# One fp32 product per batch, written straight into its layout, in place of a product per head pair that transfers rearrange: attention and two MLPs on one core

## The chip, the cores and the metric

One Trainium2 chip, one core. The metric is the device time in microseconds (us) of one launch. Three runs of the kernel before give the median that later times are compared with; the profile is one further execution. A measurement of this kernel tells differences of about 0.2% (1.4 us) from no change.

## The reference, cut to what matters

```python
B, H, S, Ns, D = 4, 8, 512, 32, 64
scores = x @ state.T / sqrt(D);  a = softmax(scores)        # 512 x 32 for each batch and head
xread = a @ state                                           # 512 x 64
scores2 = state @ x.T / sqrt(D); a2 = softmax(scores2)
sread = a2 @ x                                              # 32 x 64
x = concat([xread, sread]) -> (B * 544, 512)                # 2176 rows, all heads side by side
h = x @ w_in;  x = softplus(h) @ w_out                      # 512 -> 2048 -> 512
h = x @ w_in2; y = (max(h, 0) + alpha * min(h, 0)) @ w_out2 # 512 -> 2048 -> 512
```

## The kernel before, in words

The kernel never forms `xread`. Since xread @ w_in = a @ (state @ w_in), it makes for each batch b (4) and each quarter g of the first MLP's 2048 columns (512 columns, 4 quarters) a matrix M(b, g) = state @ w_in: 256 rows (8 heads of 32 states) by 512 columns. A tile `step1(g, b, fc)` (token `ugbf` of the program) then multiplies 128 columns of M by the attention `at` of the batch (6 matmuls of 128x128x512 into a PSUM bank `ph`), and after softplus (line 582) and a split (253, 254) the result goes through the second weights `wo` in 12 more matmuls of the same size into the four banks `pa`. There are 64 such tiles; the 128 rows of `sread` take a path of their own (`S`), and a second MLP follows (`second_mlp`), with 7 products instead of 8 by a Strassen-like scheme.

All large matmuls are in fp32r, in three passes: each operand is kept as a rounded high half and the low rest. `split` makes the two: ScalarE (ACT) copies to fp32r (line 253), VectorE (DVE) subtracts (line 254). Weights arrive as 64-bit words and are decoded by two ACT and two DVE passes per chunk (`decode`, lines 322 to 328).

How M is made before: for each quarter g and each pair of heads c, `heads_of_m` (token `hgc`) multiplies the split states of all four batches (`stm`) by the split weights `wi`: six matmuls 64x128x512 (line 546) into the two banks `px`; ACT copies both to `tf` (line 551). `make_m` (token `mbg`) then moves the rows of one batch with four transfers from `tf` to `mt` or `mu`, so that a batch's heads come to lie below each other, and splits the result into one of three slots `m` (`NM = 3`). Only M(0, 0) is made otherwise, by `make_first_m` (token `F`): eight fp32 matmuls of 64x32x512, one for each head, each with its own 64 rows and 32 columns of TensorE's array, straight into the layout of M, from weights that are decoded but not split (`wf`):

```python
for c in range(KC):
    for e in range(2):
        T.matmul(PH[ps[e]][32 * c:32 * c + 32, :], state_of(0, c, e), wf(c)[64 * e:64 * e + 64], start=True, stop=True)
```

The scores of a batch (token `s`, line 432) are made in the same form. Line 451 turns them, the softmax runs on DVE and ACT (454 to 461 and 482 to 486), lines 470 and 503 turn them again, and line 517 reads `sread`.

What sets the order: a string `PROGRAM` lists the steps. Each step adds its instructions to a graph with an estimated cost, and `Graph.order` emits them engine by engine, by due times that are worked out backward from TensorE's (PE's) list. Where that plan has PE idle at the start, it puts in filler matmuls with the identity (line 1048). On the chip every engine then runs its own list strictly in order. All transfers are issued from SyncE's queue (SP).

Of the kernel before, what the change touches and what calls it, by code (L numbers as in the profile page):

```python
# [22 lines left out]
P = 128  # L23
# [3 lines left out]
NG = 4  # L27
# [4 lines left out]
NGS = 3  # L32
NM = 3
NST = 3
# [156 lines left out]
def dve_us(n, fast=False):  # L191
    return n / (1920.0 if fast else 960.0) + 0.069
# [3 lines left out]
def attention_then_mlps_kernel(ctx: ExitStack, tc: tile.TileContext, xT, xn, st, w1i, w1o, w2i, w2o, alpha, out):  # L196
# [23 lines left out]
    AT = [lambda b=b: part(f"at{b}", None, F32R) for b in range(B)]  # L220
    STM = part("stm", None, F32R, 1024)
    SR = part("sr", None, F32R, 1024)
    MB = [lambda i=i: part(f"m{i}", None, F32R) for i in range(NM)]
    TF = part("tf", None, F32, 4096)
    MF = [part(t, None, F32, 1024) for t in ("mt", "mu")]
# [15 lines left out]
    def ring(name, n):  # L241
        count[name] = count.get(name, -1) + 1
        return count[name] % n
# [37 lines left out]
    chunk = [0] * (2 * NG)  # L281
    first_in = []

    def wf(c):
        return WF()[:, c * FW:(c + 1) * FW]

    def weight_chunk(g):
        c = chunk[g]
        chunk[g] += 1
        if c < KC:  # L290
            src, dst, key = w1i[c * P:(c + 1) * P, g * FW:(g + 1) * FW], [lambda j=j, c=c: wi_ap(g, j)[:, c, :] for j in range(2)], ("wi", g % 2, c)
        else:
            c -= KC
            src, dst, key = w1o[(g * FC + c) * P:(g * FC + c + 1) * P, :], [wo_ap(g, j)[:, c, :] for j in range(2)], ("wo", g % 2, c)
        extra = chunk[g] - 1 if g == 0 and chunk[g] > NST and chunk[g] <= KC else None
        whole = g == 0 and key[0] == "wi"
        fk = ("wi", 1, c, "hi")
        floats, fks = decode(src, extra, c if whole else None)[:2]
        if whole:
            first_in.append(lambda: split(dst[0], dst[1], lambda: wf(c), 512, [fk], [key]))  # L300
        else:
            split(dst[0], dst[1], floats, 512, fks, [key],
                  also=[("wi", 1, x, "hi") for x in range(KC)] if key[:2] == ("wi", 1) and g == 1 else [])

# [9 lines left out]
    def decode(src, extra=None, whole=None):  # L314
# [12 lines left out]
              [q(2), q(3)], [q(0), q(1)])  # L327
        G.add(DVE, dve_us(512), lambda: V.scalar_tensor_tensor(out=words()[:, :, 1] if whole is None else wf(whole).bitcast(U32), in0=words()[:, :, 1], scalar=3,
                                                              in1=words()[:, :, 0], op0=ALU.logical_shift_left, op1=ALU.bitwise_or),
              [q(0), q(1), q(2), q(3)], [q(2), q(3)] if whole is None else [("wi", 1, whole, "hi")])  # L330
        return floats, [q(2), q(3)], lambda: t().bitcast(F32).rearrange("p (f t) -> p f t", t=2)[:, :, 0], [q(0), q(1)]
# [42 lines left out]

    stm = STM.rearrange("p (j c f) -> p j c f", j=2, c=KC)
    stf = XF[B].rearrange("p (c f) -> p c f", c=KC)
    srt = SR.rearrange("p (j c f) -> p j c f", j=2, c=KC)
    att = lambda b: AT[b]().rearrange("p (j h s) -> p j h s", j=2, h=2)

    def load_state():  # L380
        load(stf, st, [("xf", B)], nbytes=P * 2048)

    def state_of(b, c, e):
        return stf[64 * e:64 * e + 64, c, 32 * (b ^ c):32 * (b ^ c) + 32]

    def split_state():
        split(stm[:, 0], stm[:, 1], stf, 512, [("xf", B)], [("stm",)])

# [9 lines left out]
    def attention(b):  # L398
# [26 lines left out]
        def scores():  # L425
# [8 lines left out]

            G.add(PE, 1.2, mm, xtk + [("xf", B)], [ps[0][1], ps[1][1]], load=0.7)
            for e in range(2):
# [71 lines left out]
        def read():  # L508
# [10 lines left out]

            G.add(PE, 2.4, mm, xsk + szk[2:], [pk], load=0.24)  # L520
            for e in range(2):
# [16 lines left out]

    def heads_of_m(g, c):
        banks = [ring("px", 2) for _ in range(2)]  # L540

        def mm():
            for k, (x, y) in enumerate(PAIRS):
                for e in range(2):
                    r = slice(64 * e, 64 * e + 64)
                    T.matmul(PX[banks[e]], stm[r, x, c, :], wi_ap(g, y)[r, c, :], start=k == 0, stop=k == 2)  # L546

        G.add(PE, 3 * MM + 0.24, mm, both(("stm",), ("wi", g % 2, c)), [("px", i) for i in banks])
        for e in range(2):
            dst = TF[:, (2 * c + e) * 512:(2 * c + e + 1) * 512]  # L550
            G.add(ACT, act_us(512, True), lambda dst=dst, i=banks[e]: A.activation(dst, PX[i], AF.Copy), [("px", banks[e])], [("tf", c, e)])  # L551

    def make_m(b, g):
        s = mslot[b, g] = ring("m", NM)
        if (b, g) == (2, 0):
            G.add(SP, 0.0, lambda: None, [], both(*[("m", s, x, y) for x in range(2) for y in range(2)]))
        i = ring("mf", 2)
        mf = MF[i].rearrange("p (h f) -> p h f", h=2)
        tf = TF.rearrange("p (c h f) -> p c h f", c=KC, h=2)
# [3 lines left out]
        for hg in range(2):  # L563
            split(lambda hg=hg: m_ap(s)[:, 0, hg, :], lambda hg=hg: m_ap(s)[:, 1, hg, :], mf[:, hg, :], 512, [("mf", i, hg, q) for q in range(4)],
                  [("m", s, hg, 0), ("m", s, hg, 1)])

    def make_first_m():
        s = mslot[0, 0] = ring("m", NM)
        ps = [ring("ph", 2) for _ in range(2)]
# [123 lines left out]
    def claim(name, keys):  # L693
        if name not in claimed:
# [8 lines left out]
    srk = both(*[("sr", b, j) for b in range(B) for j in range(2)])  # L703
    XS = [("wi0_0", wik(0, 0)), ("wi1_0", wik(0, 1)), ("wo0_0", wok(0, 0)), ("wo1_0", wok(0, 1)), ("at0", atk(0)), ("tf", [("tf", c, e) for c in range(KC) for e in range(2)]),
          ("at1", atk(1)), ("xf0", [("xf", 0, c) for c in range(KC)])]
# [5 lines left out]
    TS["u"] = [("st0", [("st", 0, k) for k in range(4)]), ("st1", [("st", 1, k) for k in range(4)])]  # L711
    TT = [("sbb", [("st", NST - 1, k) for k in range(4)]), ("sr", srk), ("mt", [("mf", 0, x, q) for x in range(2) for q in range(4)])]

# [296 lines left out]
    def run(plan):  # L1010
        units = [c for c in plan.split() if c[0] == "u"]
        n = -1
        for c in plan.split():
            if c[0] == "z":
                convert()
            elif c[0] == "w":
                weight_chunk(int(c[1]))
            elif c == "F":
                make_first_m()
            elif c[0] == "v":  # L1020
                first_in.pop(0)()
            elif c[0] == "m":
                make_m(int(c[1]), int(c[2]))
            elif c[0] == "h":
                heads_of_m(int(c[1]), int(c[2]))
            elif c[0] == "t":
                load_state()
            elif c[0] == "p":
                split_state()
            elif c[0] == "X":  # L1030
# [24 lines left out]

PROGRAM = "w0 n w0 w0 t0 w0 F v0 w0 p0 i0 j0 s0 h00 v0 w0 v0 r0 c0 l1 u000 s1 k0 u001 u002 w0 h02 b0 v0 w1 u003 h03 x0 h01 c1 r1 w0 w1 b1 x1 l2 m10 u100 m20 u101 s2 r2 c2 u102 u103 w1 b2 u200 m30 x2 h12 l3 s3 c3 r3 w1 u201 w1 u202 u203 u300 b3 h13 x3 u301 h10 u302 z u303 w1 h11 S0 w1 m01 u010 w2 u011 m11 u012 w1 u013 u110 S1 w3 u111 w2 w2 m21 z w2 w2 u112 z m31 u113 u210 z z h22 h23 u211 u212 u213 w2 u310 u311 h20 u312 u313 h21 m02 w2 m12 z u020 w3 z u021 m22 u022 u023 u120 w2 w3 u121 z w3 u122 u123 u220 z m32 w3 h33 S2 u221 u222 h30 u223 u320 h32 u321 z h31 m03 u322 u323 z u030 z z w3 u031 w3 m13 z u032 u033 w3 u130 u131 u132 m23 u133 z u230 u231 z m33 u232 z u233 u330 u331 z u332 S3 X0 u333"

# [25 lines left out]
```

## Time and profile before

| | us |
|---|---|
| runs before the change | 723.72, 724.17, 724.36 (median 724.17) |
| the profiled execution | 725.4 |
| its span, first to last instruction | 723.4 |
| PE busy in it | 710.9 |
| ACT busy, DVE busy | 434.7, 494.1 |

A row of a timeline gives start, duration, engine, line, and output and input by the program's names. Matmuls overlap, so a busy PE is not the same as a PE at its full rate; the chain of work that ended last gives the time that each piece added. Two matmul records belong to one fp32 matmul.

### The profile page before, as it was taken

What the parts mean: (1) busy time and instruction counts of PE and PEld (TensorE: products, weight loads), DVE (VectorE), ACT (ScalarE), POOL (GpSimd) and SP (SyncE); (2) the same over time, 40 slices, a digit from 0 to 9 for tenths busy, and PEclk for the clock granted to TensorE, in tenths of its full rate; (3) what the DMA queues carried; (4) which work ended last, traced back from release to release, by engine and by line L of the source; (5) the groups of instructions that cost most, each with busy time, mean ns of one, the idle gap of its engine ahead of it and who ended that gap; (6) DMA issues with size and microseconds to landing.
All of it is one profiled execution on the core that took longest, in us unless ns stands there. A gap on an engine that the chain in (4) does not pass through costs nothing.

```text
span 723.4 us, 10597 instructions
## 1 busy us (share of the span) xinstructions
PE 710.9 (98%) x3794; PEld 599.9 (83%) x3794; DVE 494.1 (68%) x931; ACT 434.7 (60%) x857; POOL 0.7 (0%) x6
## 2 busy tenths in 40 slices
PE   9989999999999999999999999999999999999995
PEld 7866777877888778888899888888899888888884
DVE  5978686676798587888798767844655764555451
ACT  6889898766876686675475655433434542443341
POOL 0000000000000000000000000000000000000000
PEclk9989999999999999999999999999999999999998
DMA  8657437555775687487479965555754545665632
GB/s 302 229 165 215 133 107 215 153 160 179 215 213 164 213 252 233 158 274 266 136 254 334 328 214 188 198 207 193 230 193 159 209 171 192 244 248 201 222 116 73
DMA packets 48872, 147.50 MB, mean 204 GB/s; under 512 B 7092, under 2 KB 21684, under 8 KB 42164
## 3 DMA queue, kind: packets, MB, share of 16 engines
q1 hardware_dynamic: 48820, 146.83, 61.0%
q8 instruction: 30, 0.49, 0.3%
q14 instruction: 22, 0.18, 0.1%
HBM read 111.42 MB, written 27.53 MB: 192 GB/s over the span
## 4 chain that ended last, share of the span: by engine, by line
PE 89%; DVE 5%; ACT 3%; DMA 1%; issue 1%; SPq 0%; DVEq 0%; ACTq 0%
PE pa L263 42%; PE ph L263 35%; PE px L263 9%; PE px L546 2%; DMA stg<-in_moe_w_in 1%; DVE n_gs L942 1%; DVE n_wo L891 0%; PE px L503 0%; DVE tmp L884 0%; PE px L470 0%; DVE small L482 0%; PE px L517 0%; PE px L432 0%; DVE wi L254 0%; ACT tf L551 0%
## 5 line engine op out<-in xcount | busy, mean ns | idle before, releaser
L263 PE MATMUL pa<-gs,wo 128*128 128x512 f32 x768 | 189.9, 397 | 0.2 <-ACT gs L253 0.2
L263 PEld LDWEIGHTS pa<-gs,wo 128*128 128x128 f32 x768 | 143.5, 190 | 34.9 <-issue 4.7
L882 ACT ACTIVATE n_gs<-n_gs 128x384 f32<-128x384 f32 (+1 forms) x96 | 48.8, 508 | 103.5 <-DVE tmp L884 67.3
L263 PE MATMUL ph<-at,m 128*128 128x512 f32 x384 | 97.2, 396 | 0.0
L263 PEld LDWEIGHTS ph<-at,m 128*128 128x128 f32 x384 | 71.0, 188 | 18.3 <-issue 2.4
L263 PE MATMUL pa<-n_m,n_wo 128*128 128x512 f32 x288 | 78.2, 393 | 0.0
L263 PEld LDWEIGHTS pa<-n_m,n_wo 128*128 128x128 f32 x288 | 53.0, 188 | 8.3
L254 DVE TENSOR_TENSOR gs<-tmp,gs 128x512 fp32r<-128x512 f32 x64 | 44.0, 689 | 22.5 <-PE pa L263 17.5
L582 ACT ACTIVATE tmp<-ph 128x512 f32<-128x512 f32 x68 | 40.4, 601 | 23.0 <-PE ph L263 20.7
L253 ACT ACTIVATE gs<-tmp 128x512 fp32r<-128x512 f32 x64 | 40.4, 635 | 22.0 <-PE pa L263 21.6
L942 DVE TENSOR_TENSOR n_gs<-ph,n_z 128x384 f32<-128x384 f32 (+1 forms) x72 | 36.2, 524 | 23.8 <-PE ph L263 21.5
L884 DVE SCALAR_TENSOR_TENSOR tmp<-n_st,nalpha,n_gs 128x384 f32<-128x384 f32 (+1 forms) x72 | 42.4, 588 | 9.0 <-ACT n_st L883 7.2
L325 DVE SCALAR_TENSOR_TENSOR st<-st 128x512 uint32<-128x512 uint32 x45 | 31.1, 691 | 16.7 <-ACT st L324 16.2
L263 PE MATMUL pa<-n_at,n_m 128*128 128x512 f32 x144 | 39.8, 392 | 0.0
L263 PE MATMUL pa<-n_at,n_at 128*128 128x512 f32 x144 | 39.7, 393 | 0.0
L891 DVE TENSOR_TENSOR n_wo<-tmp,n_wo 128x384 fp32r<-128x384 f32 (+1 forms) x48 | 25.6, 532 | 19.6 <-ACT n_wo L889 14.9
L889 ACT ACTIVATE n_wo<-tmp 128x384 fp32r<-128x384 f32 (+1 forms) x48 | 23.9, 503 | 23.5 <-PE pa L263 9.5
L942 DVE TENSOR_TENSOR n_z<-ph,n_z 128x384 f32<-128x384 f32 (+1 forms) x36 | 19.0, 527 | 27.5 <-PE ph L263 27.0
L263 PE MATMUL ph<-n_wi,n_wi 128*128 128x384 f32 (+1 forms) x192 | 37.2, 329 | 0.2 <-DVE n_gs L942 0.2
L263 PE MATMUL ph<-n_wo,n_wi 128*128 128x384 f32 (+1 forms) x186 | 35.6, 329 | 0.0
L263 PEld LDWEIGHTS ph<-n_wi,n_wi 128*128 128x128 f32 x192 | 32.9, 188 | 2.9 <-DVE n_gs L942 0.7
L883 ACT ACTIVATE n_st<-n_gs 128x384 f32<-128x384 f32 (+1 forms) x72 | 35.0, 486 | 0.1
(234 smaller groups left out, 1221.7 us busy)
## 6 DMA issues: line engine op xcount, KB each, us to landing
n_wi<-w2i SPq DMA_DIRECT2D x16, 1024.0 KB, 5.2
w2i<-z SPq DMA_DIRECT2D x56, 256.0 KB, 3.3
n_at<-w2o SPq DMA_DIRECT2D x12, 1024.0 KB, 4.8
n_m<-w2o SPq DMA_DIRECT2D x12, 1024.0 KB, 4.8
n_wi<-w2i SPq DMA_DIRECT2D x16, 768.0 KB, 4.8
st<-in_moe_w_out SPq DMA_DIRECT2D x23, 512.0 KB, 4.8
st<-in_moe_w_in SPq DMA_DIRECT2D x22, 512.0 KB, 5.0
w2o<-z SPq DMA_DIRECT2D x32, 256.0 KB, 3.9
```

The source lines that it names most:

```text
L253: G.add(ACT, act_us(n, psum), lambda: A.activation(now(hi), now(src), AF.Copy), r, k + [x for x in also if x not in k])
L254: G.add(DVE, dve_us(n), lambda: V.tensor_tensor(out=now(lo), in0=now(src), in1=now(hi), op=ALU.subtract), list(r) + k, [x + ("lo",) for x ...
L263: T.matmul(acc, lhs[x], rhs[y], start=first and (x, y) == (0, 0), stop=last and len(part) - 1 == k and len(part) != 2)
L325: G.add(DVE, dve_us(512), lambda: V.scalar_tensor_tensor(out=words()[:, :, 0], in0=words()[:, :, 1], scalar=0x80000000, in1=words()[:, :, ...
L546: T.matmul(PX[banks[e]], stm[r, x, c, :], wi_ap(g, y)[r, c, :], start=k == 0, stop=k == 2)
L582: G.add(ACT, act_us(512, True), lambda: A.activation(TMP[i], h, AF.Softplus), [hk], [("tmp", i)], table="softplus")
L882: G.add(ACT, act_us(nt, psum), lambda: A.activation(cut(r), now(h), AF.Relu), [hk] + ro + list(own), [rk])
L883: G.add(ACT, act_us(nt, psum), lambda: A.activation(cut(m), now(h), AF.Relu, scale=-1.0), [hk] + mo + list(own), [mk])
L884: G.add(DVE, dve_us(nt), lambda: V.scalar_tensor_tensor(out=cut(g), in0=cut(m), scalar=nalpha[:, c:c + 1], in1=cut(r), op0=ALU.mult, op1=A ...
L889: G.add(ACT, act_us(nt, False), lambda: A.activation(hi()[:, sl], cut(g), AF.Copy), [gk, own1], [key + ("hi",)] + ([k for k in both(*[("f" ...
L891: G.add(DVE, dve_us(nt), lambda: V.tensor_tensor(out=lo()[:, sl], in0=cut(g), in1=hi()[:, sl], op=ALU.subtract), [gk, own1, key + ("hi",)] ...
L942: G.add(DVE, dve_us(nt), lambda: V.tensor_tensor(out=dst()[:, :nt], in0=h, in1=z()[:, :nt], op=ALU.add), [hk, zk] + own, [dk])
```

## The change

- `make_m` now does for all 16 pairs (b, g) what `make_first_m` did for one: eight fp32 matmuls of 64x32x512 from the unsplit states `stf` and the decoded, unsplit weights `wf` of the quarter, into two `px` banks (for M(0, 0) `ph`), and a split from PSUM. `heads_of_m`, `split_state`, the tiles `tf`, `mt`, `mu` and `stm`, and the 60 transfers go.
- The first weights of every quarter are decoded into `wf` (for the quarters 1 to 3 a tile `wf1`); their halves, which only the `S` steps still read, are made by a step of their own (token `vg`).
- `NM` is 5, so five M can be there at once.
- `PROGRAM` is written anew; it begins `w0 i0 w0 t0 j0 w0 w0 w0 s0` where it was `w0 n w0 w0 t0 w0 F v0 w0 p0 i0 j0 s0`. The load of `alpha` (`n`) comes later.

```diff
-NM = 3
+NM = 5
...
-    WF = lambda: part("wi0_1", "wf")
+    WF = [lambda: part("wi0_1", "wf"), lambda: part("wf1")]
...
-        whole = g == 0 and key[0] == "wi"
+        whole = key[0] == "wi"
...
-    def heads_of_m(g, c):
-        banks = [ring("px", 2) for _ in range(2)]
-
-        def mm():
-            for k, (x, y) in enumerate(PAIRS):
-                for e in range(2):
-                    r = slice(64 * e, 64 * e + 64)
-                    T.matmul(PX[banks[e]], stm[r, x, c, :], wi_ap(g, y)[r, c, :], start=k == 0, stop=k == 2)
...
     def make_m(b, g):
         s = mslot[b, g] = ring("m", NM)
...
-        for c in range(KC):
-            q = b ^ c
-            load(mf[32 * c:32 * c + 32], tf[32 * q:32 * q + 32, c], [("mf", i, hg, c) for hg in range(2)], [("tf", c, hg) for hg in range(2)], nbytes=32 * 4096, cost=0.6)
...
+        tag, banks = ("px", PX) if b or g else ("ph", PH)
+        ps = [ring(tag, 2) for _ in range(2)]
 
         def mm():
             for c in range(KC):
                 for e in range(2):
+                    T.matmul(banks[ps[e]][32 * c:32 * c + 32, :], state_of(b, c, e), wf(g, c)[64 * e:64 * e + 64], start=True, stop=True)
...
         for e in range(2):
+            split(lambda e=e: m_ap(s)[:, 0, e, :], lambda e=e: m_ap(s)[:, 1, e, :], banks[ps[e]], 512, [(tag, ps[e])], [("m", s, e, 0), ("m", s, e, 1)], psum=True)
```

Three places in the lists of the engines show how the order moves. First SP's queue at the start of the program; `st`, `stg` and `stx` are staging tiles of the first weights' chunks, `xt` is the first batch's x, `xf` (before) and `stf` (after) the states. Before:

```order
L271 DMA st_80<-in_moe_w_in 128x512
L271 DMA nalpha<-in_moe_alpha 128x16x1
L271 DMA stg_123<-in_moe_w_in 128x512
L271 DMA st_79<-in_moe_w_in 128x512
L271 DMA xf_69<-in_st 128x512
L271 DMA stx<-in_moe_w_in 128x512
L271 DMA xt_116<-in_xT 128x1024 x2
```

After:

```order
L269 DMA st_77<-in_moe_w_in 128x512
L269 DMA xt_113<-in_xT 128x1024
L269 DMA stg_120<-in_moe_w_in 128x512
L269 DMA stf<-in_st 128x512
L269 DMA xt_113<-in_xT 128x1024
L269 DMA st_76<-in_moe_w_in 128x512
L269 DMA stx<-in_moe_w_in 128x512
```

The load of `alpha` has left the second place (it is now the eleventh transfer), and the two halves of x come before the last two weight chunks.

Second, PE from the turn of the first batch's scores to the first tile. `L1048` and `L1013` are the filler pairs, `L470`/`L466` make the columns, `L499` is the turn for `sread`. Before:

```order
L451 MATMUL pa_99<-ident,x2t_65 128x128 x4
L1048 MATMUL pa_102<-ident 128x128 x27
L470 MATMUL pa_100<-ident,x2t_65 128x128 x4
L470 MATMUL pa_101<-ident,x2t_65 128x128 x4
L1048 MATMUL pa_102<-ident 128x128 x13
L263 MATMUL ph_95<-at_317,m_247 128x512 x6
```

After (of the eight rows of a product of line 545 one or two stand here):

```order
L1013 MATMUL pa_99<-ident 128x128 x16
L545 MATMUL px_94<-wf,stf 32x512
...
L545 MATMUL ph_92<-wf,stf 32x512
...
L1013 MATMUL pa_99<-ident 128x128 x8
L499 MATMUL px_94<-ident,x2t_65 128x128 x4
L1013 MATMUL pa_99<-ident 128x128 x2
L466 MATMUL pa_97<-ident,x2t_65 128x128 x4
...
L1013 MATMUL pa_99<-ident 128x128 x4
L261 MATMUL ph_93<-at_309,m_284 128x512 x6
```

Two products M, a third one behind the last `L499`, and the turns for `sread` now stand ahead of the first tile, with 33 filler pairs where there were 40.

Third, ACT behind the softplus of the first tiles. `tmp` is a softplus, `gs` the high half made of it. Before:

```order
L582 ACTIVATE tmp_82<-ph_96 128x512
L253 ACTIVATE gs_0_87<-tmp_81 128x512
L582 ACTIVATE tmp_83<-ph_95 128x512
L484 ACT_TABLE_LOAD
L484 ACTIVATE xf_66,small_94<-xf_66,small_94 128x512
...
L551 ACTIVATE tf<-px_97 128x512
...
L324 ACTIVATE stg_123<-stg_123 128x512
L253 ACTIVATE gs_1_89<-tmp_82 128x512
```

After:

```order
L553 ACTIVATE tmp_78<-ph_92 128x512
L251 ACTIVATE wo_0_72<-st_76 128x512
L251 ACTIVATE gs_0_84<-tmp_78 128x512
L251 ACTIVATE wo_0_72<-stg_120 128x512
L251 ACTIVATE gs_1_86<-tmp_79 128x512
L553 ACTIVATE tmp_80<-ph_92 128x512
L553 ACTIVATE tmp_78<-ph_93 128x512
L251 ACTIVATE gs_2_88<-tmp_80 128x512
```

Before, the exponentials of the second batch (L484), copies to `tf` and decodes stand between the softplus of the second tile and its half `gs_1`, 19 instructions in all; now the halves of three tiles stand within six rows and the second batch's softmax comes behind them.

## Rows read from the trace of the kernel before

**Rows 1.** The profile page: busy time of PE and the others; then PE in 40 slices.

```profile
PE 710.9 (98%) x3794; PEld 599.9 (83%) x3794; DVE 494.1 (68%) x931; ACT 434.7 (60%) x857; POOL 0.7 (0%) x6
PE   9989999999999999999999999999999999999995
```

**Rows 2.** Stretches of the span: busy us of each engine, granted clock, DMA share, GB/s.

```profile
0.00:28.12 28.12, 26.57 (x224) 24.30 (x225) 19.21 (x41) 18.53 (x34) 0.70 (x6) 1.00 0.87 300
28.12:62.56 34.44, 31.22 (x271) 22.32 (x270) 25.22 (x53) 31.20 (x57) 0.00 (x0) 0.90 0.51 157
62.56:110.00 47.44, 47.44 (x374) 35.88 (x373) 37.43 (x87) 42.22 (x81) 0.00 (x0) 1.00 0.52 153
110.00:346.85 236.85, 236.85 (x1056) 188.93 (x1055) 181.39 (x309) 170.84 (x320) 0.00 (x0) 1.00 0.66 206
```

**Rows 3.** Timeline of PE, from the start to a read.

```profile
7.44 5.52 PE L1048 MATMUL pa<-ident 128*128 128x128 f32 x48
15.10 1.09 PE L432 MATMUL pa<-xt,xf 64*32 64x512 f32 x16
15.99 1.06 PE L574 MATMUL ph<-wf,xf 64*32 64x512 f32 x16
28.12 1.64 PE L263 MATMUL ph<-at,m 128*128 128x512 f32 x6
35.91 1.53 PE L263 MATMUL pa<-gs,wo 128*128 128x512 f32 x6
44.30 1.94 PE L517 MATMUL px<-xs,x2t 128*32 128x64 f32 x64 [1.21 <-ACT tf L551]
```

**Rows 4.** The chain that ended last, 62.56 to 112 us: start, us that it added.

```profile
64.10 1.02 PE px L432 x16
65.12 2.97 PE ph L263 x12
80.93 1.03 PE px L517 x64
85.12 0.90 PE px L546 x6
86.02 1.80 PE pa L263 x7
93.39 5.25 PE pa L263 x23
98.63 0.87 PE px L470 x8
```

**Rows 5.** Timeline of ACT and DVE: passes in pairs, late halves, first tiles.

```profile
17.19 1.27 DVE L482 TENSOR_REDUCE small<-x2t 128x1 f32<-128x512 f32 x2
17.41 1.09 ACT L253 ACTIVATE m<-ph 128x512 fp32r<-128x512 f32 x2
22.88 0.39 DVE L460 RECIPROCAL small<-small 128x16 f32<-128x16 f32 x2
24.51 0.68 DVE L254 TENSOR_TENSOR m<-ph,m 128x512 fp32r<-128x512 f32 x1
33.52 0.62 ACT L582 ACTIVATE tmp<-ph 128x512 f32<-128x512 f32 x1
35.16 1.28 ACT L484 ACT_TABLE_LOAD   x1
41.96 0.69 ACT L322 ACTIVATE st<-st 128x512 uint32<-128x512 uint16 x1
42.52 0.69 ACT L324 ACTIVATE st<-st 128x512 f32<-128x512 f32 x1
45.75 0.65 ACT L253 ACTIVATE gs<-tmp 128x512 fp32r<-128x512 f32 x1
```

**Rows 6.** Timeline of SP: the load that follows `alpha`.

```profile
1.65 2.90 SPq L271 DMA_DIRECT2D stg<-in_moe_w_in  x1
```

**Rows 7.** Stretches as in 2: PE behind the wait for `gs_1`.

```profile
42.00:44.00 2.00, 0.96 (x5) 0.48 (x5) 1.74 (x4) 2.00 (x5) 0.00 (x0) 1.00 0.16 35
46.00:48.00 2.00, 1.79 (x16) 1.26 (x5) 2.00 (x6) 1.98 (x3) 0.00 (x0) 0.50 0.50 111
```

**Rows 8.** The copies to `tf`: the group by line, then its share of a stretch.

```profile
L551 ACT ACTIVATE tf<-px 128x512 f32<-128x512 f32 x32 | 17.2, 592 | 4.1 <-PE px L546 4.1
...
0.00:110.00 110.00, 6.42 (x12) 0.97 0.60 192
```

**Rows 9.** The chain as in 4, output matmuls from 46.45 us on.

```profile
46.45 2.07 PE pa L263 x4
48.74 2.63 PE pa L263 x7
```

More of the change, by code (lines that the diff above doesn't have):

```diff
@@ L281, in attention_then_mlps_kernel, with wf, wf_key @@
     chunk = [0] * (2 * NG)
-    first_in = []
-    def wf(c):
-        return WF()[:, c * FW:(c + 1) * FW]
+    halves_in = [[] for _ in range(NG)]
+    def wf(g, c):
+        return WF[g > 0]()[:, c * FW:(c + 1) * FW]
+    def wf_key(g, c):
+        return ("wf", c) if g else ("wi", 1, c, "hi")
     def weight_chunk(g):
@@ L295, in weight_chunk @@
         extra = chunk[g] - 1 if g == 0 and chunk[g] > NST and chunk[g] <= KC else None
-        whole = g == 0 and key[0] == "wi"
-        fk = ("wi", 1, c, "hi")
-        floats, fks = decode(src, extra, c if whole else None)[:2]
+        whole = key[0] == "wi"
+        also = [("wi", 1, x, "hi") for x in range(KC)] if g == 1 else []
+        floats, fks = decode(src, extra, (g, c) if whole else None)[:2]
         if whole:
-            first_in.append(lambda: split(dst[0], dst[1], lambda: wf(c), 512, [fk], [key]))
+            halves_in[g].append(lambda: split(dst[0], dst[1], lambda: wf(g, c), 512, [wf_key(g, c)], [key], also=also))
         else:
-            split(dst[0], dst[1], floats, 512, fks, [key],
-                  also=[("wi", 1, x, "hi") for x in range(KC)] if key[:2] == ("wi", 1) and g == 1 else [])
+            split(dst[0], dst[1], floats, 512, fks, [key])
     stages = [0, NST]
@@ L327, in decode @@
               [q(2), q(3)], [q(0), q(1)])
[L328 removed]
+        G.add(DVE, dve_us(512), lambda: V.scalar_tensor_tensor(out=words()[:, :, 1] if whole is None else wf(*whole).bitcast(U32), in0=words()[:, :, 1], scalar=3,
                                                               in1=words()[:, :, 0], op0=ALU.logical_shift_left, op1=ALU.bitwise_or),
[L330 removed]
+              [q(0), q(1), q(2), q(3)], [q(2), q(3)] if whole is None else [wf_key(*whole)])
         return floats, [q(2), q(3)], lambda: t().bitcast(F32).rearrange("p (f t) -> p f t", t=2)[:, :, 0], [q(0), q(1)]
@@ L433, in mm @@
                                  start=True, stop=True)
[L435 removed]
+            G.add(PE, 1.07, mm, xtk + [("stf",)], [ps[0][1], ps[1][1]], load=0.7)
             for e in range(2):
@@ L537, in m_ap @@
         return MB[i]().rearrange("p (j h f) -> p j h f", j=2, h=2)
-    def heads_of_m(g, c):
-        banks = [ring("px", 2) for _ in range(2)]
-        def mm():
-            for k, (x, y) in enumerate(PAIRS):
-                for e in range(2):
-                    r = slice(64 * e, 64 * e + 64)
-                    T.matmul(PX[banks[e]], stm[r, x, c, :], wi_ap(g, y)[r, c, :], start=k == 0, stop=k == 2)
[L548 to L551, printed above, removed]
     def make_m(b, g):
         s = mslot[b, g] = ring("m", NM)
-        if (b, g) == (2, 0):
+        if 4 * g + b == NM - 1:
             G.add(SP, 0.0, lambda: None, [], both(*[("m", s, x, y) for x in range(2) for y in range(2)]))
-        i = ring("mf", 2)
-        mf = MF[i].rearrange("p (h f) -> p h f", h=2)
-        tf = TF.rearrange("p (c h f) -> p c h f", c=KC, h=2)
-        for c in range(KC):
-            q = b ^ c
-            load(mf[32 * c:32 * c + 32], tf[32 * q:32 * q + 32, c], [("mf", i, hg, c) for hg in range(2)], [("tf", c, hg) for hg in range(2)], nbytes=32 * 4096, cost=0.6)
[L563 to L569, printed above, removed]
+        tag, banks = ("px", PX) if b or g else ("ph", PH)
+        ps = [ring(tag, 2) for _ in range(2)]
         def mm():
@@ L573, in mm @@
                 for e in range(2):
-                    T.matmul(PH[ps[e]][32 * c:32 * c + 32, :], state_of(0, c, e), wf(c)[64 * e:64 * e + 64], start=True, stop=True)
-        G.add(PE, 1.2, mm, [("xf", B)] + [("wi", 1, c, "hi") for c in range(KC)], [("ph", i) for i in ps], load=0.7)
+                    T.matmul(banks[ps[e]][32 * c:32 * c + 32, :], state_of(b, c, e), wf(g, c)[64 * e:64 * e + 64], start=True, stop=True)
+        G.add(PE, 1.1, mm, [("stf",)] + [wf_key(g, c) for c in range(KC)], [(tag, i) for i in ps], load=0.7)
         for e in range(2):
-            split(lambda e=e: m_ap(s)[:, 0, e, :], lambda e=e: m_ap(s)[:, 1, e, :], PH[ps[e]], 512, [("ph", ps[e])], [("m", s, e, 0), ("m", s, e, 1)], psum=True)
+            split(lambda e=e: m_ap(s)[:, 0, e, :], lambda e=e: m_ap(s)[:, 1, e, :], banks[ps[e]], 512, [(tag, ps[e])], [("m", s, e, 0), ("m", s, e, 1)], psum=True)
     def softplus(h, hk):
@@ L703, in attention_then_mlps_kernel @@
     srk = both(*[("sr", b, j) for b in range(B) for j in range(2)])
-    XS = [("wi0_0", wik(0, 0)), ("wi1_0", wik(0, 1)), ("wo0_0", wok(0, 0)), ("wo1_0", wok(0, 1)), ("at0", atk(0)), ("tf", [("tf", c, e) for c in range(KC) for e in range(2)]),
+    XS = [("wi0_0", wik(0, 0)), ("wi1_0", wik(0, 1)), ("wo0_0", wok(0, 0)), ("wo1_0", wok(0, 1)), ("at0", atk(0)), ("wf1", [("wf", c) for c in range(KC)]),
           ("at1", atk(1)), ("xf0", [("xf", 0, c) for c in range(KC)])]
@@ L711, in attention_then_mlps_kernel @@
     TS["u"] = [("st0", [("st", 0, k) for k in range(4)]), ("st1", [("st", 1, k) for k in range(4)])]
-    TT = [("sbb", [("st", NST - 1, k) for k in range(4)]), ("sr", srk), ("mt", [("mf", 0, x, q) for x in range(2) for q in range(4)])]
+    TT = [("sbb", [("st", NST - 1, k) for k in range(4)]), ("sr", srk), ("m3", mkeys(3))]
     def slot(entry, dtype=F32R, n=2048, use="n"):
```

23 lines of the change are left out of this document (6 added, 17 removed).

## The prediction

> **What bounds the kernel now.** I read the page first: TensorE (PE) is busy for 710.9 of 723.4 us and has a full slice nearly everywhere [rows 1]. So the time is PE's own work, plus what PE loses at the start and the end. The stretches say where it loses [rows 2]: from 62.56 us to the second MLP PE is busy for every microsecond at full clock. Before 62.56 us it looks busy too, but in the first 28.12 us nearly all of it is filler with the identity, and from 28.12 to 62.56 us it is idle for 3.2 us and runs at a mean clock of 0.90. A gain must therefore come from the first 62.56 us or from less PE work behind them. The timeline shows what the start waits for [rows 3]: first tile at 28.12, first output matmul at 35.91, and then a long stretch in which ScalarE (ACT) is late. The softplus of the second tile ends at 34.14, but ACT makes its high half only at 45.75, because a table load, the second batch's exponentials, copies to `tf` and decodes stand between them [rows 5]. PE is half idle meanwhile and then gets half the clock [rows 7]. From 62.56 to 110 us ACT is busy for 42.2 of 47.4 us and PE does not stall [rows 2]: ACT is close to the bound there, not over it.
>
> **Prices of PE's pieces**, as the chain adds them [rows 4]: an output matmul 5.25 / 23 = 0.228 us; the turn into columns 0.87; the read for `sread` 1.03; a product per head pair (line 546) 0.90, and the seven matmuls behind it took 1.80 instead of 7 x 0.228 = 1.60, so 1.10 in all. The new product exists already in two places of this trace, as `make_first_m` and, in the same form, as the scores: 1.02, and the twelve matmuls behind it took 2.97 instead of 2.74, so 1.25 in all.
>
> "True FP32: 4 passes through PE array" says the Trainium skill (FP8 and Floating Point Precision, TensorE Precision Notes), which speaks against fp32 where three fp32r passes stood. My estimate by it: 512 columns x 4 at 2.4 GHz are 0.85 us a matmul, 6.8 us for eight one after another, and 16 products would cost over 90 us more. The trace shows all eight in 1.02 us, so the eight tiles of the array do run side by side; I take the row.
>
> **The change, walked along the engines' new lists** with durations of the rows. In pairs a DVE pass over 512 columns takes 1.27, one alone 0.68, so passes follow each other at 0.60; ACT passes at 0.50 from PSUM and 0.56 from SBUF [rows 5].
>
> *Scores.* Ahead of them PE has 42 filler matmuls instead of 48 and ten, and nothing else. A filler takes 5.52 / 48 = 0.115 us [rows 3], so they start at 7.44 + 42 x 0.115 = 12.3 instead of 15.10. The data should be there: x's second half is the fifth transfer, no longer the eighth, and the load of `alpha`, behind which SP was held for 2.90 us [rows 6], now comes later.
>
> *First tile.* The first row maximum began 2.09 us behind the scores (17.19 against 15.10) [rows 3, 5], so now at 14.4. From there DVE's list up to the last low half of `at` holds 23 passes of 512 columns and nine small ones: 23 x 0.60 + 0.9 = 14.7 (the small ones at 0.1, from a pair of reciprocals in 0.39 [rows 5]; an estimate). The tile can run from 29.1 to 30.5; it ran from 28.12 to 29.76. So nothing is won up to here except what PE has behind it by then: three products M and the turn for `sread`.
>
> *First output matmul.* ACT reaches the second half of `at` at about 27.0, by the same walk; from 27.6 to the first `gs` there are six passes from SBUF, six from PSUM and a table load: 3.4 + 3.0 + 1.28 = 7.7, so `gs` is there at 35.9. On PE the fourth tile waits for the fourth of these PSUM passes (34.8), then come 1.38 for the tile and 1.02 for the scores: first output matmul at 37.2 instead of 35.91. Late so far by 1.3 us.
>
> *The 48 output matmuls.* Now the halves of the first three tiles follow each other on ACT ahead of the second batch's softmax, so PE has input. Up to the second batch's first tile it does 42 of them (9.6), the turn of the scores with a wait for its copies (0.9 + 0.7), the read with what it delays (1.25), the columns (0.9), two turns (1.0), a small turn with a wait (0.5) and 0.2 of waits for DVE: 15.0, to 52.2. The missing six, the second read and its turn are 2.8 more: 55.0. The kernel before has the same behind it at 62.56. That is **7.6 us earlier**, and the three products M of the first quarter are done, as the four pairs of heads were.
>
> *What is left then.* Twelve products at 1.25 against twelve pairs of heads at 1.10: **+1.8**. The later halves of weights, ACT's and DVE's splits of M (0.60 against 0.68 a pass) and the decodes lie beside a PE that is the bound, with ACT busy 72% of 110 to 346.85 us and DVE 77% [rows 2]. If that cover were gone, the 24 splits of the twelve products would cost 0.5 each, 12 us. What falls away there, 32 copies of 17.2 us on ACT [rows 8] and 60 transfers with a DMA share of 0.66 [rows 2], is hidden work and I give it nothing; the 12 copies ahead of 110 us [rows 8] relieve a busy ACT, which is in the walk already.
>
> *A new wait.* The two `px` banks of a product were free when ACT had copied them; now they are free when DVE has subtracted too. The smallest drain is 0.36 from PE to ACT (M(0, 0) ended at 17.05, its copy began at 17.41 [rows 3, 5]), 0.50 to ACT's second pass, 0.60 for that and 0.68 for DVE: 2.1 us. In the third quarter four products stand 10 to 12 matmuls apart, 2.3 to 2.8 us. Every pass ahead of theirs in a queue makes PE wait, and all output matmuls behind wait too. The trace has no such case; below it is 0, above one pass (0.6) for each of twelve products, 7.2. I take 0.3 for each of the four closest, **+1.0** with rounding, since the lists put the splits at the head of what becomes ready.
>
> Sum: -7.6 + 1.8 + 1.0 = **-4.8 us**. Against the profiled execution 725.4 - 4.8 = 720.6; that execution stands 1.2 over the median, so for the median 724.17 - 4.8 = **719.4 us**.
>
> Bounds: the product at the price of a pair of heads (1.10) gives 1.8 back; at 1.40 (its busy 1.09 [rows 3] and 0.3) it costs 1.8 more. The walk is uncertain by about 1.5 either way, the waits that I added to it.
>
> **Rivals.**
> 1. *The clock falls.* From 23 to 29 us PE's new list has turns, 18 filler matmuls and one product, with waits. Behind a mixture of turns, products and waits the granted clock was 0.50 [rows 7]; there 11 output matmuls added 4.7 instead of 2.5 us [rows 9] and a read took 1.94 instead of 1.03 [rows 3], 3.1 us in all. The same at the first tiles leaves a gain of 1.7: 722.5 us. The fillers speak against it, which the stretch at 42 us had not. [...]
> 2. *The banks drain too late* (slower). At 0.6 us of wait for each of the twelve late products the sum becomes -7.6 + 1.8 + 7.2 = +1.4: 725.6 us. It decides from 5.8 / 12 = 0.48 us a product on. For it speaks that before, DVE took the second low half of M(0, 0) at 24.51, 7.5 us behind the product's end [rows 3, 5]; against it, that the bank was not wanted there.
> 3. *The second batch is late instead.* In the walk its `at` is ready 0.5 us before PE wants it, and DVE works without a break from 14.4 to 51. Any microsecond that DVE loses there is PE's. With 5 us of such slips the gain is gone and the change only moves the wait: 724 us.
> 4. *More than the walk shows.* If my waits in the walk don't come up and the products cost no more than the pairs, 719.4 - 1.5 - 1.8 - 1.0 = 715.1 us.
>
> **How the numbers follow.** Forecast (717.2 to 721.2) 0.58; clock 0.12; banks 0.09; moved wait 0.08; more 0.13. A measurement here tells 0.2% (1.4 us) from nothing. Faster by more: 0.58 + 0.12 + 0.13 = 0.83; within: 0.08; slower: 0.09. The range 715.0 to 723.0 leaves out the banks, most of the moved wait and little of the last case. Alone, the likeliest case has 717.2 to 721.2.
>
> **What the profile after would show.** PE's chain adds about 1.02 us for each product of line 545, 0.2 more in the piece behind; scores at 12.3; first tile near 29; first output matmul near 37 and no hole behind it; ACT's second and third `gs` within 3 us of the first; PE's last idle time before 56 us; full clock from 29 us on. Wrong I would be if PE waits for ACT or DVE at line 545 in the later quarters, if the clock is 0.50 in a stretch between 24 and 40 us, or if x or a weight chunk lands after its engine is ready.

## The result and the profile after

| | before | after |
|---|---|---|
| median of the runs, us | 724.26 (723.72 to 725.04, 4 runs) | 717.12 (716.32 to 717.40, 4 runs) |
| ratio | | 0.9899, 95% interval 0.9882 to 0.9916 |
| the profiled execution, its span | 725.4, 723.4 | 716.91, 714.7 |

The change makes the kernel 7.1 us faster; 4.8 were forecast (719.4, range 715.0 to 723.0). The two profiled executions lie 8.7 us apart in their spans, mostly since that of the kernel before (725.4) stands 1.1 us above its median; what follows compares these two. The page of the changed kernel, busy time and PE's slices, against [rows 1]:

```profile
PE 706.0 (99%) x3918; PEld 590.0 (83%) x3918; DVE 490.3 (69%) x930; ACT 417.2 (58%) x824; POOL 0.7 (0%) x6
PE   9999999999999999999999999999999999999996
```

Stretches of the changed kernel (busy us of PE, PEld, DVE, ACT, POOL; granted clock; DMA share; GB/s), against [rows 2]:

```profile
0.00:28.12 28.12, 26.70 (x236) 22.45 (x237) 18.65 (x39) 18.53 (x34) 0.70 (x6) 1.00 0.82 290
28.12:56.00 27.88, 27.81 (x274) 20.11 (x273) 24.78 (x54) 26.50 (x49) 0.00 (x0) 1.00 0.48 155
56.00:110.00 54.00, 53.83 (x409) 41.32 (x408) 44.29 (x97) 49.37 (x95) 0.00 (x0) 1.00 0.45 147
```

In the stretch behind the first tile PE is busy for all but 0.07 us at full clock; before, it was idle for 3.2 us and had 0.90. ACT is busy for 26.5 of 27.9 us there: it has almost no air left, which the experiments will use. The timeline of PE, against [rows 3]:

```profile
11.82 1.09 PE L428 MATMUL pa<-xt,stf 64*32 64x512 f32 x16
18.63 1.09 PE L545 MATMUL px<-wf,stf 64*32 64x512 f32 x16
28.30 1.63 PE L261 MATMUL ph<-at,m 128*128 128x512 f32 x6
36.67 2.12 PE L261 MATMUL pa<-gs,wo 128*128 128x512 f32 x8
50.55 1.64 PE L261 MATMUL ph<-at,m 128*128 128x512 f32 x6
```

The last row is the second batch's first tile. 42 output matmuls stand between it and the first output matmul; with the six that are missing, the read and its turn (2.8 us, as in the prediction) the common point is at 50.55 + 2.8 = 53.3 us, against 62.56: 9.2 us earlier. The rest of the span is 714.7 - 53.3 = 661.4 against 723.4 - 62.56 = 660.8. So the gain is made in the first 53 us, and on balance 0.6 us of it are given back behind them. ACT's halves `gs` there, against [rows 5]:

```profile
34.43 0.66 ACT L251 ACTIVATE gs<-tmp 128x512 fp32r<-128x512 f32 x1
35.50 0.66 ACT L251 ACTIVATE gs<-tmp 128x512 fp32r<-128x512 f32 x1
36.98 0.67 ACT L251 ACTIVATE gs<-tmp 128x512 fp32r<-128x512 f32 x1
```

The second half follows the first by 1.07 us; before the change it came at 45.75, 11.75 behind the first. And this is a part of the chain that ended last, ahead of the first tile's softplus (start, us that it added):

```profile
24.75 0.60 ACT at L251
25.34 0.97 ACT x2t L502 x2
26.32 0.49 ACT at L251
26.81 0.59 ACT stg L322
27.39 0.56 ACT stg L324
27.95 0.97 ACT m L251 x2
28.93 0.55 ACT wo L251
29.48 0.51 ACT st L322
```

One ACT pass after the other, decodes and a product's copies among them. From 17.94 us to the end of that softplus at 32.56 us the chain stands on ACT, apart from short gaps; ahead of it, from 13.63 us, it stands on DVE, and behind it on PE. So the start is now a queue of DVE and then of ACT.

### The profile page after: what moved, and what is told of

It is laid out like the page before. It is cut to its first block, busy times and chain, and to the rows that moved or that the text cites. A ratio compares the mean times of both kernels' runs of the same rounds, so it can differ in the third digit from the quotient of the medians.

```text
span 714.7 us, 10685 instructions
## 1 busy us (share of the span) xinstructions
PE 706.0 (99%) x3918; PEld 590.0 (83%) x3918; DVE 490.3 (69%) x930; ACT 417.2 (58%) x824; POOL 0.7 (0%) x6
## 4 chain that ended last, share of the span: by engine, by line
PE 93%; ACT 3%; DVE 2%; issue 1%; POOLq 0%; POOL 0%; ACTq 0%; DVEq 0%
PE pa L261 42%; PE ph L261 35%; PE px L261 9%; PE px L545 2%; PE pa L1012 1%; PE pa L1013 1%; PE px L513 1%; PE px L428 0%; ACT m L251 0%; PE px L499 0%; PE px L466 0%; DVE n_gs L913 0%; DVE xf L566 0%; PE px L625 0%; PE px L447 0%
## 5 line engine op out<-in xcount | busy, mean ns | idle before, releaser
L261 PE MATMUL pa<-gs,wo 128*128 128x512 f32 x768 | 187.3, 394 | 0.2 <-ACT x2t L569 0.2
L853 ACT ACTIVATE n_gs<-n_gs 128x384 f32<-128x384 f32 (+1 forms) x96 | 48.6, 506 | 108.9 <-DVE tmp L855 67.5
```

Source lines behind the costliest of these rows:

```text
L261: T.matmul(acc, lhs[x], rhs[y], start=first and (x, y) == (0, 0), stop=last and len(part) - 1 == k and len(part) != 2)
L853: G.add(ACT, act_us(nt, psum), lambda: A.activation(cut(r), now(h), AF.Relu), [hk] + ro + list(own), [rk])
```

## The experiments

Two theories were put against each other. **A**: the gain comes from the order, above all on ACT, where the halves of the first tiles stand ahead of the second batch's softmax. **B**: it comes from the product's form, which needs no copies to `tf` and no transfers. Each kernel ran beside runs of the kernel before, whose median moved between 723.9 and 724.7; so each difference is to the runs of the kernel before that stood beside it. The changed kernel has -7.1.

| run | median, us | to the kernel before | ratio, 95% interval |
|---|---|---|---|
| e2, new product, old order | 721.88 | -2.9 | 0.9961, 0.9948 to 0.9973 |
| e3, old product, new order | 726.55 | +1.8 | 1.0026, 1.0014 to 1.0038 |
| e6, second batch's scores first | 721.31 | -3.4 | 0.9951, 0.9939 to 0.9964 |
| e9, ACT's copies twice, first quarter | 721.72 | -2.2 | 0.9965, 0.9953 to 0.9978 |
| e12, e6 and e9 together | 725.09 | +0.4 | 1.0004, 0.9995 to 1.0014 |
| e10, ACT's copies twice, later quarters | 718.93 | -5.0 | 0.9930, 0.9917 to 0.9944 |
| e4, every product twice | 730.34 | +5.6 | 1.0072, 1.0057 to 1.0088 |
| e5, no planned fillers | 716.98 | -7.0 | 0.9898, 0.9884 to 0.9911 |
| e7, fewer fillers in front | 717.45 | -6.5 | 0.9909, 0.9896 to 0.9923 |
| e1, `alpha` in second place | 717.29 | -7.4 | 0.9896, 0.9881 to 0.9911 |
| e11, halves of weights later, planned anew | 724.11 | -0.6 | 0.9991, 0.9982 to 1.0000 |
| e13, the same halves moved by hand | 719.27 | -5.1 | 0.9930, 0.9916 to 0.9944 |

**e2: the new product in the old order** of the first quarter (heads and split states left out of the program, the later halves put in; from `m01` on as after).

```diff
-PROGRAM = "w0 i0 w0 t0 j0 w0 w0 w0 s0 w0 w0 m00 v0 r0 m10 c0 l1 b0 w0 k0 m20 m30 s1 u000 w1 v0 w1 n x0 w1 u001 c1 w1 u002 r1 u003 ..."
+PROGRAM = "w0 n w0 w0 t0 w0 m00 v0 w0 i0 j0 s0 v0 w0 v0 r0 c0 l1 u000 s1 k0 u001 u002 w0 b0 v0 w1 u003 x0 c1 r1 w0 w1 b1 x1 l2 m10 u100 m20 ..."
```

> The new product with the old order of the first quarter: the program as before up to the last tile of the first quarter, with the heads and transfers left out and the later halves of weights put in, then the program of the changed kernel. Theory A (the gain comes from ACT's list: halves of the first tiles ahead of the second batch's softmax): here the softmax of the second batch and a table load stand between the second and the third half, so most of the loss at the start stays and the time is 721 to 724.5 us; PE is idle or at half clock somewhere between 36 and 50 us. Theory B (the gain comes from the product itself: no copies to tf on ACT, no transfers, fewer passes): 717 to 718.5 us.

721.88, inside A's window: the product alone brings 2.9 of the 7.1 us. The half clock that A allowed for did not show: PE kept full clock from 28 us on. It was idle for 1.1 us of 40 to 50 us, 0.7 of that waiting for `gs`:

```profile
46.69 0.73 PE L261 MATMUL pa<-gs,wo 128*128 128x512 f32 x2 [0.66 <-ACT gs L251]
```

**e6: the converse, within the new product.** Only the place of two products in the program moves.

```diff
-... w0 k0 m20 m30 s1 u000 w1 v0 w1 n x0 w1 u001 c1 w1 u002 r1 u003 ...
+... w0 k0 s1 u000 m20 w1 v0 w1 n x0 w1 u001 c1 m30 w1 u002 r1 u003 ...
```

> The changed kernel with one thing moved back: the second batch's scores stand ahead of the products M(2,0) and M(3,0) in the program, so that its exponentials come between the softplus of the first tile and its half on ACT. Same work on every engine. Theory A: 3 to 7 us of the gain are given back, 720 to 724 us. Theory B: no change, 716.5 to 718 us.

721.31, inside A's window: 3.7 us of the gain are given back, though the two kernels have the same operations to do, fillers aside. The reason stands in the timelines of e6, ACT first, then PE:

```profile
32.59 1.28 ACT L480 ACT_TABLE_LOAD   x1
33.89 0.72 ACT L480 ACTIVATE xf<-xf,small 128x512 f32<-128x512 f32 x1
41.58 0.65 ACT L251 ACTIVATE gs<-tmp 128x512 fp32r<-128x512 f32 x1
...
35.23 2.05 PE L1013 MATMUL pa<-ident 128*128 128x128 f32 x16
38.25 1.16 PE L1013 MATMUL pa<-ident 128*128 128x128 f32 x8
42.38 2.54 PE L261 MATMUL pa<-gs,wo 128*128 128x512 f32 x10
```

Because PE makes the second batch's scores ahead of the two products, at 27.11 us instead of 35.65, its table load and exponentials come between the first softplus and its half; PE does filler instead, and the first output matmul starts at 42.38 instead of 36.67. That is 5.7 us later, of which 2.0 come back, since the second batch's own work is done earlier: its first tile runs at 45.87 instead of 50.55.

**e3: the order alone, with the old product.** The pairs of heads stand ahead of the tiles, and an edge in the plan holds the second batch's scores behind the fourth tile.

```diff
-G.add(PE, 1.2, mm, xtk + [("xf", B)], [ps[0][1], ps[1][1]], load=0.7)
+G.add(PE, 1.2, mm, xtk + [("xf", B)] + ([("tile",)] if b == 1 else []), [ps[0][1], ps[1][1]], load=0.7)
...
-... l1 u000 s1 k0 u001 u002 w0 h02 b0 v0 w1 u003 h03 x0 h01 c1 r1 ...
+... l1 k0 w0 b0 v0 h02 h03 h01 u000 u001 u002 w1 u003 s1 x0 c1 r1 ...
```

> The old product by pairs of heads, transfers and all, with only the order changed: the pairs of heads of the first quarter ahead of the first tiles, and the second batch's scores held behind the fourth tile, so that ACT makes the first three halves within a few instructions and the second batch's exponentials come behind them. Theory A: most of the gain is there without the new product, 717 to 720 us, ACT's second and third gs within 4 us of the first, no stretch at half clock behind 30 us. Theory B: 723 to 726 us.

726.55, slower than before and just above B's window. Theory A in its plain form falls. The timeline of ACT in e3 shows that the order did what it should, three halves within 6.2 us (4 were expected) and no softmax between them; the waits of PE (us in total, times, longest) and one stretch show where it was lost:

```profile
34.69 0.65 ACT L253 ACTIVATE gs<-tmp 128x512 fp32r<-128x512 f32 x1
39.30 0.69 ACT L253 ACTIVATE gs<-tmp 128x512 fp32r<-128x512 f32 x1
40.88 1.22 ACT L253 ACTIVATE gs<-tmp 128x512 fp32r<-128x512 f32 x2
...
PE px L503 <- DVE at L254: 2.4, 2, 1.8
PE pa L263 <- ACT x2t L598: 2.3, 1, 2.3
...
50.00:56.00 6.00, 4.03 (x14) 2.98 (x14) 5.91 (x11) 5.61 (x10) 0.00 (x0) 0.72 0.63 156
```

ACT still has the copies to `tf` to make and DVE is full too, so the second batch's `at` is late in place of the first batch's `gs`: PE waits at 51 and 52 us, has a mean clock of 0.72, and waits again at 67.5 us. The order only moved the lateness, as rival 3 of the prediction describes it. In this order all eight copies to `tf` of the first quarter stand ahead of the first output matmul; in the kernel before it was two. A new theory, **A2**: the order pays only together with the passes that the new form takes off ACT at the start.

**e9: those passes put back.** In `split` the ACT copy is issued `times` times; the plan and all lists stay.

```diff
-lambda: A.activation(now(hi), now(src), AF.Copy), r, k +
+lambda: [A.activation(now(hi), now(src), AF.Copy) for _ in range(times)], r, k +
...
-[("m", s, e, 0), ("m", s, e, 1)], psum=True)
+[("m", s, e, 0), ("m", s, e, 1)], psum=True, times=2 if g == 0 else 1)
```

> The changed kernel, with ACT's copy of both banks issued twice in the split of the four products of the first quarter: 8 passes of 0.5 us more on ACT ahead of 35 us, as many as the copies to tf that the kernel before had in its first quarter; PE's work and all lists else are the same. Theory A2 (the gain needs the order and the passes that the new form takes off ACT at the start): 2 to 4 us more than the changed kernel, 719 to 721 us, the first output matmul at 39 instead of 36.67. Theory B2 (only the order counts; those passes are hidden): at most 0.7 us more, 717 to 718 us.

721.72, a little above A2's window. The 8 passes last 5.0 us and not 4 (ACT is busy for 422.2 us, with 417.2 in the changed kernel), and they cost 4.9 us: all that they last. PE's waits for ACT in e9, and its first output matmul, 4.6 us later than 36.67:

```profile
PE px L545 <- ACT x2t L502: 1.3, 1, 1.3
PE ph L261 <- ACT tmp L553: 1.3, 2, 1.1
PE px L499 <- ACT x2t L480: 1.2, 2, 0.8
...
41.29 2.12 PE L261 MATMUL pa<-gs,wo 128*128 128x512 f32 x8
```

**e12: both undone at once**, the edits of e6 and e9 in one kernel.

> Both parts of the explanation undone at once, in the new product: the second batch's scores moved ahead of M(2,0) and M(3,0), and ACT's copies of the first quarter's four products issued twice. Alone they gave back 4.2 and 4.6 us of 717.1. Theory A2 (these two are the gain, and the product's form brings nothing beside them): 723 to 727 us, the time of the kernel before or a little more. Rival (both prices are one and the same wait, seen twice): 720 to 722.5 us.

725.09, +0.4 to the kernel before: 7.5 us more than the changed kernel, where 3.7 and 4.9 add up to 8.6. With these two undone the new product has the time of the old kernel. A2 stands; that both are one wait seen twice (720 to 722.5 us) is out.

**e10: the cover of the later products.** As e9, with `times=2 if g else 1`.

> The same doubling for the twelve products of the later quarters alone: 24 passes of 0.5 us more on ACT, and each px bank free 1.0 us later. If ACT's and DVE's work of the later products lies beside a PE that is the bound, as the prediction has it: 0 to 0.5 us more. If that cover were gone, or the banks drain late: up to 12 us more; PE would wait for DVE or ACT at line 545.

718.93, between the two windows: 24 passes, 12.8 us more of ACT's time (430.0 against 417.2 us), cost 2.1. The chain of e10 shows the products that paid; the other eight stay at 1.02:

```profile
121.44 1.34 PE px L545 x16
165.76 1.82 PE px L545 x16
170.49 1.37 PE px L545 x16
174.81 1.34 PE px L545 x16
```

Their excess over 1.02 is 0.32 + 0.80 + 0.35 + 0.32 = 1.8. These are the four products that follow 10 or 12 matmuls behind the last one. As the kernel stands, their banks drain in time, but with little to spare: in the changed kernel DVE's second low half ends 0.4 to 0.9 us before the next of these products starts.

**e4: every product twice**, each matmul issued two times into the same place.

```diff
-T.matmul(banks[ps[e]][32 * c:32 * c + 32, :], state_of(b, c, e), wf(g, c)[64 * e:64 * e + 64], start=True, stop=True)
+[T.matmul(banks[ps[e]][32 * c:32 * c + 32, :], state_of(b, c, e), wf(g, c)[64 * e:64 * e + 64], start=True, stop=True) for _ in range(2)]
```

> Each of the eight matmuls of every product is issued twice in a row into the same place (same result, same order of everything else); it prices the product. By the row of 1.02 us, of which some 0.9 to 1.0 are added again where PE is dense (twelve late products, one of the first four): 11 to 13 us more, 728 to 730 us. If the eight tiles ran one after another (6.8 us a product, an estimate from the Trainium skill's rule of four passes in FP8 and Floating Point Precision, TensorE Precision Notes), it would be over 80 us more.

730.34, 12.7 us over the changed kernel. Its chain at a late product and the piece behind it, and the same place in the changed kernel:

```profile
172.97 1.92 PE px L545 x32
174.90 2.94 PE pa L261 x12
```

```profile
165.21 1.02 PE px L545 x16
166.22 2.94 PE pa L261 x12
```

Eight more matmuls add 0.90 us, twelve times 10.8 of the 12.7. The Trainium skill has "4 passes through PE array" for true fp32 (FP8 and Floating Point Precision, TensorE Precision Notes); the prediction's estimate by it, for eight matmuls one after another, was 6.8 us a product. The trace does not agree with one after another: in the changed kernel the 240 records of line 545 into `px` last 601 ns each and keep PE busy for 16.8 us together, so they lie side by side. The piece behind a product has 12 x 0.228 + 0.2 = 2.94 both times: that surcharge belongs to the change of form, not to the number of matmuls.

**e5 and e7: the fillers.** e5 sets `G.filler = lambda: None`; e7 leaves out the first 16 planned pairs.

> The changed kernel without the 59 pairs of filler matmuls that the plan puts in (the 32 matmuls with the identity at the very start stay). If the fillers hold the clock: a granted clock of 0.50 in stretches between 12 and 45 us, and 2 to 6 us more, 719 to 723 us. If they do nothing: 716.5 to 717.5 us.

> The changed kernel without the first 16 pairs of planned fillers, 32 matmuls ahead of the first scores; by the fillers' rate (4.85 us for 42) they could start up to 3.7 us earlier, if x were there. If x lands near 9.9 us (issued at 2.6, 7.3 to land) the scores start at 10.0 to 10.5 instead of 11.82; if all behind them follows, 0.6 to 1.5 us less, 715.6 to 716.5. If DVE's chain is tied to the weight chunks and not to the scores: no change within 0.4 us.

716.98 and 717.45: no change that this measurement tells, in either. The fillers do hold the clock, but where nothing hangs on it. e5 has a mean clock of 0.73 from 12 to 28.35 us (first row), and its product at 26.35 us takes 2.07 us, where that at 25.89 us of the changed kernel takes 1.57; yet its first tile is at 28.35 and its first output matmul at 37.39, 0.05 and 0.7 us later than with fillers. e7's scores (last row) wait for x, which lands at 11.1 and not at 9.9:

```profile
12.00:28.35 16.35, 12.88 (x81) 5.37 (x72) 15.31 (x34) 13.24 (x27) 0.00 (x0) 0.73 0.81 291
...
37.39 2.13 PE L261 MATMUL pa<-gs,wo 128*128 128x512 f32 x8
...
11.11 1.09 PE L428 MATMUL pa<-xt,stf 64*32 64x512 f32 x16 [2.76 <-DMA xt<-in_xT]
```

**e1: the load of `alpha`**, moved back (`w0 n i0` for `w0 i0`, and the later `n` gone).

> The changed kernel with the load of alpha back in the second place of SP's queue; all other lists are the same. If SP is held behind it as before the change (2.9 us), x's second half is issued at 5.5 instead of 2.6 and lands near 14 instead of 11.1: scores at 14 instead of 11.82 and 1.5 to 2.5 us more, 718.6 to 719.6. If what lands first is set by the bytes and not by the queue's order: 716.8 to 717.6.

717.29, no change. The scores start 0.6 us later, and these 0.6 us stay up to the end of the span (715.3 against 714.7), which is less than the medians can tell. SP is held behind `alpha` again, now with the first half of x (first row), and the scores wait 0.24 us for x (second row):

```profile
1.65 3.07 SPq L269 DMA_DIRECT2D xt<-in_xT  x1
...
12.44 1.09 PE L428 MATMUL pa<-xt,stf 64*32 64x512 f32 x16 [0.24 <-DMA xt<-in_xT]
```

**e11 and e13: an attempt to go on.** If ACT's passes at the start cost their time, those that nobody needs early should go. The halves of the first weights (token `v`) are only read by the `S` steps. e11 holds them back by an edge in the plan (the first `v` tokens of `PROGRAM` move back with it), and the plan then orders everything anew:

```diff
-split(dst[0], dst[1], lambda: wf(g, c), 512, [wf_key(g, c)], [key], also=also)
+split(dst[0], dst[1], lambda: wf(g, c), 512, [wf_key(g, c)] + ([] if g else [("tile",)]), [key], also=also)
```

> The changed kernel with the halves of the first quarter's first weights (four ACT and four DVE passes, three of each ahead of the first tile now) held until a tile has run, so that none lies ahead of the first tiles on ACT or DVE; only the late S step reads them. If ACT's and DVE's passes ahead of the first output matmuls are the bound, as the doubling of ACT's copies showed (4.6 us for 8 passes): two passes that stood between the first batch's exponentials and the rest (1.2 us on ACT, 0.6 on DVE) come back, 715 to 716.5 us. If they stood in gaps: 716.8 to 717.6.

724.11, outside both windows: nearly all of the gain is lost. The first tile runs at 28.26 as before, but the plan now pulls the second batch forward. On PE its reads and turns stand ahead of the second tile's output matmuls, and PE waits for them in order; on DVE its softmax stands ahead of the low half of the second chunk of `wo`, which was made at 36.08 and now comes at 47.12 (third row). Behind the waits the clock is 0.50 (last row, 46 to 50 us):

```profile
44.05 0.47 PE L521 MATMUL px<-ident,x2t 128*128 128x128 f32 x1 [1.36 <-DVE x2t L518]
45.83 2.12 PE L466 MATMUL px<-ident,xf 128*128 128x128 f32 x8 [1.31 <-DVE xf L457]
...
47.12 0.68 DVE L252 TENSOR_TENSOR wo<-stg,wo 128x512 fp32r<-128x512 f32 x1
...
46.00:50.00 4.00, 4.00 (x15) 3.23 (x15) 4.00 (x10) 1.66 (x3) 0.00 (x0) 0.50 0.38 74
```

e13 keeps every list and only takes these splits out and puts them in behind 70 us.

```diff
+        out = [(self.late.get(i, t), i) for t, i in out]
         out.sort(key=lambda x: (x[0], -1 if x[1] is None else x[1]))
...
+            if g < 2:
+                for k in range(2):
+                    G.late[len(G.ops) + k] = 70.0 + 16.0 * g + 4.0 * c + 0.8 * k
```

> The changed kernel with the eight splits of first weights of quarters 0 and 1 (one ACT and one DVE pass each) taken out of their places and put behind 70 us of the plan; every list else keeps its order, PE's too. Three ACT and three DVE passes then leave the time ahead of the first tile, a fourth DVE pass the time ahead of the first output matmul. If every pass there is worth its time, as with the passes that were added (4.6 us for 8): 1.0 to 2.0 us less than 717.1, so 715 to 716. If other work is then the last to be ready (the first tile 16.5 us behind the scores, as now): 716.5 to 717.5.

719.27, outside both windows and 2.0 us slower than the changed kernel. Nothing is won in front: scores at 11.51, first tile at 28.01, 16.5 us apart as before. Where the two ACT passes stood, ACT now waits for DVE (first row); they had lain in a gap. Some 0.5 us are won between 53 and 66 us. But behind 62 us, where ACT is busy for 44 of 47.5 us, the moved passes make PE wait (second row):

```profile
18.84 1.23 ACT L461 ACTIVATE x2t<-x2t 128x512 f32<-128x512 f32 x2 [2.80 <-DVE x2t L459]
...
77.44 0.33 PE L529 MATMUL px<-ident,xf 128*128 128x128 f32 x1 [1.03 <-DVE xf L526]
```

So a pass added to ACT's queue ahead of the first tile costs its time, and a pass taken away there gave nothing: in e13 the chain stands on DVE from 13.3 to 24.3 us and on ACT from 24.4 us on, so the two set the first tile together. No kernel tried here is measurably faster than the changed one.

## Why the prediction was right, point by point

- **The number**: 717.12 lies just below the likeliest case (717.2 to 721.2), inside the range. Between the two profiled executions, which the walk was made on, the forecast is some 3.9 us short (-4.8 against -8.7): the walk gave 1.6 too little gain and the rest 2.2 too much cost, and the two errors add up. Against the medians it is 2.3 short, since the profiled execution of the kernel before stood 1.1 above its median; where in the kernel these 1.1 lie is not known.
- **The bound** held: the time from the common point on is unchanged within 0.6 us, and the gain lies in the first 53 us.
- **The walk** gave 7.6 us, the trace 9.2. Scores 12.3, measured 11.82; first tile 29.1, 28.30; first output matmul 37.2, 36.67; second batch's first tile 52.2, 50.55. The largest part is in the step of the 48 output matmuls: 13.9 us where 15.0 were reckoned, because the waits in it (0.7 for the scores' copies, 0.5 and 0.2) did not come up.
- **The reason for the gain** was half of it as the prediction weighs it. That the halves come ahead of the second batch's softmax is worth 3.7 us (e6). The copies to `tf` that fall away ahead of 110 us were only said to be in the walk; put back in like number they cost 4.9 us (e9), together 7.5 (e12), and without their going the order brings nothing (e3). As far as these runs tell, the two parts together are the gain; the 60 transfers and the five slots of `NM` were not tried alone.
- **The products**: 1.25 each was forecast; the chain has 1.02 and 0.2 behind it, 1.22. e4 confirms both parts.
- **The new wait**, +1.0 (four times 0.3 is 1.2), was mis-sized: PE waits for DVE at no product; rival 2 is refuted for this spacing. Its bound was near, though: with some 1.0 us more of drain four products wait 1.8 us (e10).
- Together the rest was forecast 2.8 us dearer and is 0.6. The traces say where: at the second MLP's first matmul (346.85 us before, 339.25 after) the lead is 7.6 us, so of the 9.2 the products' 12 x (1.22 - 1.10) = 1.4 and a wait of 0.2 at 65.64 us are gone. In the second MLP, whose work the change leaves as it is, the lead grows again to 8.7 us. Two waits of the kernel before for line 942, at 420 and 452 us and 0.4 us together, are not there in the changed kernel; the cause of the other 0.7 stays open.
- **Hidden at nothing**: borne out for the later quarters as far as e10 tells, where 12.8 us of ACT's time more cost 2.1, 1.8 of them through the banks. What a pass taken away there gives back was not tried.
- **Rival 1**, the clock: it is 1.00 in both stretches behind 28 us. The fillers are not the reason that it costs nothing: without them the clock falls before the first tile and the time stays (e5), so the price of 3.1 us taken from [rows 7, 9] does not hold ahead of the first tile. From 28.35 us on e5 has full clock again, so a low clock at the output matmuls was not tried.
- **Rival 3** is what e3 shows with the old product; in the changed kernel PE does not wait for the second batch's `at`. **Rival 4** came true in its first half, the walk's waits; the products did cost more than the pairs.
- **The reasons for the earlier scores** were partly wrong: neither the place of `alpha` (e1) nor the number of fillers (e7) moves the time beyond the noise. Where PE waits for x, it lands at 10.90 (e5), 11.11 (e7) and 12.44 us (e1). e7's scores start 0.7 us earlier than the changed kernel's, and its first tile comes 0.5 us later (28.80).

## What to carry to other kernels

Where a start is a queue of an engine beside PE, take the order and the load of that engine together: a better order with the old load was slower here, the lighter load in a worse order gave less than half, and only both gave 7 us. Doubling an operation in place, with every list unchanged, prices it and shows the margin of its neighbours; but the price of an added pass is not what a removed one gives back, since another chain may be ready no earlier. And a plan that reorders by itself makes a small edit a large one (e11): compare the lists before reading the time.

## What was not expected of the hardware

- In the changed kernel the instruction that follows `alpha`'s load was held on SP's queue for 10.2 us (2.90 in [rows 6], 3.07 in e1); no engine waited for it there. In e1, where `alpha` stands second, the same transfer took 0.33 us. The timeline of SP in the changed kernel:

```profile
9.66 10.20 SPq L269 DMA_DIRECT2D st<-in_moe_w_out  x1
```

- A held queue made the data only a little late: in e1 x's second half was issued at 5.71 instead of 2.60 us and was there at 12.44, 1.3 us later than the 11.11 of e7. Why so little is lost was not tried.
- Eight fp32 matmuls in eight tiles of the array cost 0.90 us when they follow eight of the same form, 1.02 with the change into that form, and 0.2 more falls on the piece behind.
